# First layer norm as (x − mean)·(1/std) in one two-scalar instruction, 1/std by ln and exp, and a new order of all operations

## Chip, cores, metric

One core of one Trainium2 chip. The metric is the device time of one execution in microseconds (us); lower is better. Ratios of two kernels are the mean time of the one's fast runs over the mean of the other's fast runs of the same rounds, so they are not quite the ratio of the medians that stand beside them. A profiled span is about 1.8 us shorter than the time of the same execution. In lines of the profile PE is TensorE (PEld its weight loads), DVE VectorE, ACT ScalarE and POOL GpSimd; L422 is line 422 of that run's kernel; the number in square brackets is the time that the engine was idle before, and what ended it.

## The reference, cut to what matters

```python
h = _layernorm(x, axis=-1) * (1 + ca) + sa          # first norm: the change is here
x = x + ga * _A_ref(h, A_wqkv, A_w_phi, A_wo)       # linear attention, 32 heads of 16
h = _layernorm(x, axis=-1) * (1 + cb) + sb
x = x + gb * _B_ref(h, B_w_gate, B_w_up, B_w_down)  # silu-gated feed-forward, 512 -> 1376 -> 512
# sa, ca, ga, sb, cb, gb = six parts of silu(c) @ w_mod;  x is 2048 x 512, bf16
# _layernorm: (x - mean) / sqrt(var + 1e-5)
```

The attention needs K and V of all 2048 rows before the first row of its output. So the kernel has a first half (norm, K, V, the K features, their sum over all rows, Q) and a second half (attention output, projection, second norm, feed-forward), which begins when the last of 16 row tiles has gone through the K features.

## The kernel before

The program lists operations with the engines that could do each, and a long list ORDER says in which order and on which engine each is placed; the number beside an engine is the duration in us with which the search for an order reckons. Cut to the parts that matter here:

```python
def rstd_of(mv_t, n, bmv, name, bufs):                 # 1/std and -mean/std, all on GpSimd
    ...
        nc.gpsimd.tensor_scalar_add(neg[:], mv_t()[:, :, 1], LN_EPS)
        nc.gpsimd.tensor_tensor(st["rstd"][:], neg[:], mhalf[:, 0:n], op=ALU.pow)
        ...
            nc.gpsimd.tensor_scalar(neg[:], mv_t()[:, :, 0], -1.0, None, op0=ALU.mult)
            nc.gpsimd.tensor_tensor(st["nmr"][:], neg[:], st["rstd"][:], op=ALU.mult)

def normalize(src, rstd_t, bn, nmr_t, q, reads):       # x * (1/std) + (-mean/std), on one of three engines
    ...
    def fp():
        nc.gpsimd.tensor_scalar(bxn()[:], src, rstd_t()[:, q:q + 1], nmr_t()[:, q:q + 1],
                                op0=ALU.mult, op1=ALU.add)
    pl.op([("DVE*", 0.35, fd), ("ACT", 0.72, fa), ("POOL", 1.11, fp)], r=list(reads) + [bn], w=[bxn])

def k_tile(i):                                         # one row tile of K and V
    ...
    pl.op("POOL", r=[e, R], w=[bphik[i]], us=1.9, fn=lambda: nc.gpsimd.tensor_tensor(   # K features: softmax's division
        bphik[i]()..., e()..., R()[:].unsqueeze(2).to_broadcast([P, 2 * H, DH]), op=ALU.mult))

first_norm(0, 2); ...; first_norm(2, 2); ...           # groups of row tiles: 2, 2, 4, 4, 4
first_norm(4, 4)
first_T(4, 4)
later(wmod_sb[:, :, 2 * D:6 * D], wmod_v[:, :, 2 * D:6 * D])   # 2 MB in one load
```

The softmax here doesn't subtract the row's maximum and nothing guards it: scores larger than these inputs give would overflow.

## Time and profile before

| kernel | median us | lowest to highest | profiled span | clock |
|---|---|---|---|---|
| before | 215.3 (4 runs) | 214.73 to 216.17 | 213.2 | 0.997 |

TensorE bounds the kernel, except for holes in the first 30 us. The prediction shows the lines and how they are read. One more line is needed below, from the groups by shape of the kernel before (columns: line, engine, operation, operands, count, then busy us, mean ns of one, idle before):

```profile
L406 POOL TENSOR_SCALAR xn<-x_c,ln_rstd,ln_nmr 128x512 bf16<-128x512 bf16 x10 | 7.7, 769 | 0.9
```

This is GpSimd's normalization of one row tile: 769 ns.

### The profile page before, as it was taken

How to read it: one execution, taken by the hardware profiler on the slowest of the kernel's cores; microseconds unless marked ns; L12 is line 12 of the kernel's file. 1: busy time of each engine (PE TensorE's matmuls, PEld its weight loads, DVE VectorE, ACT ScalarE, POOL GpSimd, SP SyncE). 2: the span in 40 equal slices, each digit the busy share in tenths (PEclk: the TensorE clock that was granted, in tenths of full speed). 3: DMA queues.
4: the chain of work that ended last, by engine and by line, in shares of the span. 5: the costliest groups of instructions: out<-in, count | busy, mean ns of one | idle time of the engine just before them, and what ended most of it. 6: DMA issues, size and time to landing. Idle time of an engine off the chain costs nothing.

```text
span 213.2 us, 4730 instructions
## 1 busy us (share of the span) xinstructions
PE 200.7 (94%) x1779; PEld 140.2 (66%) x1807; DVE 149.8 (70%) x352; ACT 118.9 (56%) x241; POOL 115.7 (54%) x157
## 2 busy tenths in 40 slices
PE   4997789999999999998999999999999999999993
PEld 1853554555555687786867877777776687777772
DVE  5799969999686977677887596677577764532314
ACT  2677989998889873433533603443342465363230
POOL 5257998899920535672642743654584563441340
PEclk9999999999999999999999999999999999999998
DMA  6996970389600011312221121123211222010001
GB/s 195 363 350 104 389 84 20 71 285 402 217 3 0 0 28 29 74 38 39 54 49 49 39 64 31 46 51 74 52 25 49 51 50 51 28 25 26 28 25 49
DMA packets 30793, 19.24 MB, mean 90 GB/s; under 512 B 22481, under 2 KB 28082, under 8 KB 30770
## 3 DMA queue, kind: packets, MB, share of 16 engines
q1 hardware_dynamic: 30480, 18.85, 31.8%
q8 instruction: 14, 0.23, 0.5%
q10 hardware_dynamic: 290, 0.08, 0.2%
q14 instruction: 9, 0.07, 0.1%
HBM read 11.58 MB, written 2.10 MB: 64 GB/s over the span
## 4 chain that ended last, share of the span: by engine, by line
PE 77%; DMA 13%; SPq 3%; DVE 3%; issue 1%; POOL 1%; DVEq 0%; POOLq 0%
PE one_ps L869 31%; PE one_ps L904 16%; PE one_ps L642 6%; PE one_ps L817 6%; PE one_ps L590 5%; PE one_ps L586 5%; DMA wmod_sb<-in_w_mod_dram 4%; DMA wqkv_sb<-in_A_wqkv_dram 4%; PE four_ps L746 3%; SPq L318 2%; DMA raw<-xn 2%; DMA oT<-o 2%; PE kv_ps L618 2%; DMA wphi_sb<-in_A_w_phi_dram 2%; DVE x_c L820 1%
## 5 line engine op out<-in xcount | busy, mean ns | idle before, releaser
L876 ACT ACTIVATE sg<-one_ps 128x512 bf16<-128x512 f32 (+3 forms) x52 | 27.2, 529 | 44.3 <-PE one_ps L869 39.8
L869 PE MATMUL one_ps<-hT,wu_sb 128*128 128x256 bf16 (+3 forms) x440 | 45.7, 251 | 0.8 <-DVE hT L840 0.8
L869 PE MATMUL one_ps<-hT,wg_sb 128*128 128x256 bf16 (+3 forms) x440 | 44.5, 251 | 0.0
L904 PE MATMUL one_ps<-wd_sb,gu 128*128 128x512 bf16 (+3 forms) x172 | 42.0, 366 | 0.8
L869 PEld LDWEIGHTS <-wu_sb 128*128 128x128 bf16 (+1 forms) x440 | 36.9, 100 | 8.8 <-issue 0.9
L869 PEld LDWEIGHTS <-wg_sb 128*128 128x128 bf16 (+1 forms) x440 | 36.9, 100 | 7.7
L885 POOL TENSOR_TENSOR gu<-usb,sg 128x512 bf16<-128x512 bf16 (+1 forms) x22 | 22.6, 1026 | 22.8 <-ACT sg L876 15.8
L611 POOL TENSOR_TENSOR phik<-e,R 128x1024 bf16<-128x1024 bf16 x16 | 30.6, 1930 | 3.5 <-DVE R L609 2.2
L879 DVE TENSOR_TENSOR gu<-one_ps,sg 128x512 bf16<-128x512 f32 (+2 forms) x30 | 17.8, 595 | 15.9 <-PE one_ps L869 13.0
L904 PEld LDWEIGHTS <-gu 128*128 128x128 bf16 (+1 forms) x187 | 17.8, 98 | 11.9
L375 DVE BATCH_NORM_STATS2 st<-x_c 128x6 f32<-128x512 bf16 x32 | 21.2, 680 | 1.7 <-DMA x_c<-in_A_x_dram 1.4
L883 ACT CAST usb<-one_ps 128x512 bf16<-128x512 f32 (+1 forms) x22 | 11.3, 525 | 18.8 <-PE one_ps L869 15.8
L911 DVE TENSOR_TENSOR fg<-one_ps,gab 128x512 bf16<-128x512 f32 (+1 forms) x17 | 11.2, 656 | 14.8 <-PE one_ps L904 14.5
L804 POOL TENSOR_TENSOR o<-o 128x512 bf16<-128x512 bf16 x14 | 16.2, 1157 | 8.7 <-DVE o L784 8.7
L607 DVE TENSOR_REDUCE S<-e 128x64 f32<-128x1024 bf16 x16 | 19.0, 1194 | 2.2 <-ACT e L597 2.1
L784 DVE TENSOR_TENSOR o<-four_ps,A 128x512 bf16<-128x512 f32 x32 | 20.6, 684 | 0.0
L915 POOL TENSOR_TENSOR ot<-x_c,fg 128x512 bf16<-128x512 bf16 x8 | 9.2, 1154 | 18.5 <-DVE fg L911 18.5
L597 ACT ACTIVATE e<-one_ps 128x512 bf16<-128x512 f32 x32 | 17.3, 607 | 2.7 <-PE one_ps L586 1.7
L648 ACT ACTIVATE eT<-one_ps 128x512 bf16<-128x512 f32 x32 | 17.5, 644 | 1.2 <-PE one_ps L642 1.1
L817 PE MATMUL one_ps<-wo_sb,oT 128*128 128x512 bf16 x60 | 16.2, 379 | 0.5 <-DMA oT<-o 0.3
L820 DVE TENSOR_TENSOR x_c<-x_c,one_ps 128x512 bf16<-128x512 bf16 x16 | 11.0, 687 | 7.5 <-PE one_ps L817 7.2
L590 PE MATMUL one_ps<-wqkv_sb,hT 128*128 128x512 bf16 x62 | 15.8, 379 | 0.1
(102 smaller groups left out, 273.7 us busy)
## 6 DMA issues: line engine op xcount, KB each, us to landing
wmod_sb<-in_w_mod_dram SPq DMA_DIRECT2D x1, 2048.0 KB, 8.2
out_dram<-ot SPq DMA_DIRECT2D x15, 128.0 KB, 1.9
x_c<-in_A_x_dram SPq DMA_DIRECT2D x3, 512.0 KB, 9.4
wg_sb<-in_B_w_gate_dram SPq DMA_DIRECT2D x1, 1376.0 KB, 8.3
wu_sb<-in_B_w_up_dram SPq DMA_DIRECT2D x1, 1376.0 KB, 11.2
wd_sb<-in_B_w_down_dram SPq DMA_DIRECT2D x1, 1280.0 KB, 14.4
wmod_sb<-in_w_mod_dram SPq DMA_DIRECT2D x4, 256.0 KB, 5.0
wqkv_sb<-in_A_wqkv_dram SPq DMA_DIRECT2D x2, 512.0 KB, 7.8
```

What stands on the lines that cost most here:

```text
L375: pl.op("DVE", r=reads, w=[st6], us=0.6, fn=lambda: nc.vector.bn_stats(st6()[:], src))
L590: nc.tensor.matmul(v()[:], lhsT=hT[c_i][k][:, cols], rhs=wqkv_sb[:, k, 2 * D:3 * D], start=(k == 0), stop=(k == KD - 1))
L607: pl.op("DVE", r=[e], w=[Ss], us=1.14, fn=lambda: nc.vector.tensor_reduce(Ss()[:], e()[:].rearrange("p g s h f -> p (g s h) f"), axis=AX.X ...
L611: pl.op("POOL", r=[e, R], w=[bphik[i]], us=1.9, fn=lambda: nc.gpsimd.tensor_tensor(bphik[i]()[:].rearrange("p g s h f -> p (g s h) f"), e( ...
L648: pl.op("ACT", r=[pq, btab], w=[beT[c_i, sg, j]], us=0.48, fn=lambda sg=sg: nc.scalar.activation(eTs[c_i, sg, j][:], pq()[:], ACT.Exp, sca ...
L784: nc.vector.tensor_tensor(o2()[:, sg].rearrange("p j (h d) -> p j h d", d=DH), ndv()[:, :, sg, 0:P].rearrange("p j (h d) -> p j h d", d=DH ...
L817: nc.tensor.matmul(a()[:], lhsT=oT()[:, j, :], rhs=wo_sb[:, j, :], start=(j == 0), stop=(j == KD - 1))
L869: nc.tensor.matmul(ps_()[0:fsz, q * n:(q + 1) * n], lhsT=wt[:, k, m * P:m * P + fsz], rhs=h2[k], start=(k == 0), stop=(k == KD - 1))
L876: pl.op("ACT", r=[g, btab], w=[sg], us=0.08 + 0.41 * L / CW, fn=lambda: nc.scalar.activation(sg()[0:fsz, 0:L], g()[0:fsz, 0:L], ACT.Silu))
L879: pl.op("DVE", r=[u, sg], w=[gu], us=0.07 + 0.535 * L / CW, fn=lambda: nc.vector.tensor_tensor(gu()[0:fsz, 0:L], u()[0:fsz, 0:L], sg()[0:f ...
L885: pl.op("POOL", r=[usb, sg], w=[gu], us=0.05 + 1.06 * L / CW, fn=lambda: nc.gpsimd.tensor_tensor(gu()[0:fsz, 0:L], usb()[0:fsz, 0:L], sg() ...
L904: nc.tensor.matmul(fp()[:], lhsT=b()[0:fsz, c0:c0 + P], rhs=wd_sb[0:fsz, m, cs], start=(m == 0), stop=(m == FM - 1))
```

## The change

The intent: take the first norm's small instructions off GpSimd (ln and exp on ScalarE give 1/std, and no −mean/std is needed if the mean is subtracted first), take the normalizing itself off ScalarE, let row tiles 4 to 7 go on in pairs, split a 2 MB load, and search a new order with re-fitted durations. Core of the diff (QUOTA limits how many buffers of a kind the order may hold, and PAIRS lists the groups of four row tiles that go on in pairs; the 948 numbers of ORDER become 954 others; further re-fitted constants, changed fillers, the rest of the load bookkeeping and the removal of an unused path are cut):

```diff
-QUOTA = {'q': 3, 'turn': 4, 'T': 2, 'T2': 2, 'wo': 4, 'down': 3, 'gu': 2, 'kv': 4, 'fold': 4}
+QUOTA = {'q': 9, 'turn': 9, 'T': 9, 'T2': 9, 'wo': 9, 'down': 9, 'gu': 9, 'kv': 9, 'fold': 9}
+PAIRS = (0, 1)
...
+    nc.scalar.add_instruction(mybir.InstLoadActFuncSet(name=..., act_func_set_id=6, ins=[], outs=[]))
...
+    def rstd_lnexp(mv, n, bmv, name):
+        ...
+        def fa():
+            nc.scalar.activation(var[:], mv[:, :, 1], ACT.Ln, bias=eps_t[:])
+            nc.scalar.activation(rstd[:], var[:], ACT.Exp, scale=-0.5)
+        def fp():
+            nc.gpsimd.tensor_scalar_add(var[:], mv[:, :, 1], LN_EPS)
+            nc.gpsimd.tensor_tensor(rstd[:], var[:], mhalf[:, 0:n], op=ALU.pow)
+        pl.op([("ACT", 0.8, fa), ("POOL", 0.9 + 0.1 * n, fp)], r=bmv, w=[b])
+    def center(src, mv, rstd, b, q, reads):
+        ...
+        def f(eng):
+            eng.tensor_scalar(bxn()[:], src, mv[:, q, 0:1], rstd[:, q:q + 1], op0=ALU.subtract, op1=ALU.mult)
+        pl.op([("DVE*", 0.35, lambda: f(nc.vector)), ("POOL", 0.78, lambda: f(nc.gpsimd))], r=list(reads) + [b], w=[bxn])
...
-    first_norm(4, 4)
-    first_T(4, 4)
+    first_norm(4, 2)
+    first_T(4, 2)
+    first_norm(6, 2)
+    first_T(6, 2)
...
-    later(wmod_sb[:, :, 2 * D:6 * D], wmod_v[:, :, 2 * D:6 * D])
+    for i in range(2):
+        cols = slice((2 + 2 * i) * D, (4 + 2 * i) * D)
+        later(wmod_sb[:, :, cols], wmod_v[:, :, cols], [], [bm2[i]])
```

## The prediction

> **What bounds the kernel now.** I read the page's busy shares first:
>
> ```profile
> PE 200.7 (94%) x1779; PEld 140.2 (66%) x1807; DVE 149.8 (70%) x352; ACT 118.9 (56%) x241; POOL 115.7 (54%) x157
> ```
>
> TensorE is the engine to save on, but 94% includes the filler matmuls (the line L978), which only multiply ones. So the second view is the table of windows (stretch, busy us of PE, PEld, DVE, ACT and POOL with counts, clock, DMA share, GB/s):
>
> ```profile
> 10.00:20.00 10.00, 8.80 (x57) 4.59 (x59) 9.48 (x25) 7.44 (x15) 6.07 (x9) 1.00 0.93 257
> 20.00:30.00 10.00, 8.10 (x83) 5.14 (x83) 8.88 (x20) 9.09 (x16) 9.27 (x12) 1.00 0.94 251
> 40.00:50.00 10.00, 9.95 (x81) 5.28 (x81) 9.68 (x13) 10.00 (x20) 9.51 (x7) 1.00 0.79 262
> 170.00:190.00 20.00, 19.90 (x156) 15.21 (x157) 9.50 (x22) 10.96 (x21) 9.16 (x14) 1.00 0.19 41
> ```
>
> The reader is to see that from 40 us on TensorE is full, while between 10 and 30 us the other three engines are at 75 to 95% and TensorE is not. The timeline of TensorE between 15 and 31 us (start, us, engine, line, operands, count, idle before) shows what is missing:
>
> ```profile
> 15.26 0.38 PE L978 MATMUL kv_ps<-ones 128*128 128x512 bf16 x1
> 15.47 0.61 PE L419 MATMUL one_ps<-ident_b,xn 128*128 128x128 bf16 x8
> ...
> 17.84 0.40 PE L523 MATMUL one_ps<-BD,WT 128*128 128x128 bf16 x4 [1.11 <-ACT hT L427]
> 18.08 0.59 PE L978 MATMUL kv_ps<-ones 128*128 128x512 bf16 x2
> 18.51 1.03 PE L586 MATMUL one_ps<-Wk,hT 128*128 128x512 bf16 x4
> ...
> 24.36 0.61 PE L419 MATMUL one_ps<-ident_b,xn 128*128 128x128 bf16 x8
> 24.81 0.83 PE L978 MATMUL kv_ps<-ones 128*128 128x252 bf16 x6
> 27.37 0.55 PE L464 MATMUL one_ps<-silucT,wmod_sb 128*128 128x1 bf16 x16 [1.73 <-DMA wmod_sb<-in_w_mod_dram]
> ```
>
> Two holes: 15.3 to 18.5 us (tiles 2 and 3 are not yet transposed and modulated) and 23.3 to 27.4 us. In the second, row tiles 4 to 7 become usable only as a group of four, and the next matmuls in order stand behind the 2 MB second load of w_mod, issued at 19.14 and landed at 27.3. By 27.4 TensorE has done K and V of only four tiles. From there to the last matmul at 209.7 us I add up about 2.2 us of idle and 0.65 us of fillers (the waits of TensorE and three 216 ns fillers at 69 to 74 us), most of it between 68 and 99 us. The last 3.5 us are the final evacuation and store.
>
> The middle has a second limit. The timeline of GpSimd shows the K features going one after the other until the attention can start:
>
> ```profile
> 49.11 9.47 POOL L611 TENSOR_TENSOR phik<-e,R 128x1024 bf16<-128x1024 bf16 x5 [0.25 <-PE one_ps L586]
> ```
>
> That is 1.9 us a tile, 16 tiles, with little idle from 24 us on; the last key-value matmuls (57.8 to 59.1 us) wait for it. So a gain in front stays only if GpSimd is brought forward too.
>
> **What the Trainium skill says.** "ScalarE: Activation LUTs", section "Table sets: the hidden batching unit": ln and exp lie together in one named set, so going from one to the other needs no second load; its section "What ACT_TABLE_LOAD costs" gives about 1283 ns for a load. The trace agrees on the load: two, 1283 ns each (before the first exp, and before silu). The change loads one set by hand at the start; if that is the common set, the count stays two. "GPSIMD Engine Reference", section 3.1, has 769 ns measured for a one-input loop over 512 elements; GpSimd's normalize here takes 769 ns (L406, x10), so the cost model's old 1.11 us was wrong and the new 0.78 right. The same page, section 1, says GpSimd shares its SBUF interfaces with VectorE, with contention for instructions in a two-port mode; the trace shows VectorE's normalize between 314 and 405 ns, not enough to prove it.
>
> **The change part by part.** The order lists name an operation and its engine in each number; counting the operations in program order decodes them, so I could read the new order per engine. It is all rearranged, so costs are taken from present rows.
>
> (1) First norm. Now five groups each run four small GpSimd instructions: about 1.8 us for two tiles (6.90 to 8.59) and 2.0 for four, five groups 9.6 us. Afterwards six groups (tiles 4 to 7 split into pairs); two stay on GpSimd with two instructions (0.24 + 0.73 and gaps, 1.05 us each, 2.1 us), four go to ScalarE as ln and exp (about 0.8 us each by the listed cost; the 128x4 exp here takes 0.17 us, so most is hand-over). Normalizing: now 5 tiles on GpSimd, 9 on ScalarE, 2 on VectorE; afterwards 11, 0 and 5. GpSimd gets 6 x 0.77 = +4.6 us, loses 7.5 us and one modulation (0.8): net about -3.7. ScalarE loses 9 x about 0.74 = 6.7 us and gets 3.2: net -3.5. VectorE gets 3 x 0.36, about +1. The subtraction form costs the same as the multiply-add.
>
> (2) Pairs for tiles 4 to 7, x and w_mod loads in halves, new order. I walked the new order by hand. The first K matmul stays near 11.6 us (now 11.79): it waits for w_mod's first 1 MB, whose last quarter is used at 9.55. ScalarE does ln and exp of tiles 2 and 3 before the first K exponentials, 12.9 to 13.6; two exponential pairs and a V copy (1.06 + 1.06 + 0.55) end at 16.2; the two evacuations (0.97 each) at 18.2. So the first hole stays: tile 3 starts near 18.4 against 18.5. From there the new TensorE order is: four K/V (0.865 each), transposes of 6 and 7, the first key-value product, a fold, to 23.2; tile 6's evacuation on ScalarE ends near 23.0. Then K6, V7, K7 to 26.1, K4 at 26.35, and gate 0 at 27.2, which needs only the first half of w_mod (landing about 24, an estimate: half of 8.2 us after 19.6). V5, K5, V4, the modulation columns, V6 and gate 1 follow without a hole to 34.1, where K8 starts. Now K8 starts at 37.19. The work ahead of it is the same: one gate more (0.865) and one Q block less, and two modulation steps more (0.25). Sum: 37.19 - 34.1 + 0.25 = 3.3 us of holes removed.
>
> (3) GpSimd's chain by the same walk: its features of tiles 1, 3 and 2 end near 30.4, tile 4's at 34.3, then 11 x 1.93 ends near 55.5 against 58.6 now. That is 3.1 us earlier, so it follows TensorE nearly in full. Eight Q blocks precede the first attention matmul in both orders, eight follow it.
>
> (4) After that TensorE's work is the same instruction for instruction. What can still be won is the 2.85 us of idle and fillers. The new order pulls attention matmuls further ahead of their users, but the start looks alike: tile 2's output needs about 8 us from attention matmul to projection (vector work, a 1.16 us add, a 4.1 us transpose), with 7.6 us of other work placed there, a hole of about 0.4 as now (0.29). I allow 0.8 us of the 2.85 to go.
>
> (5) Removed, no effect on the end: the unused late path, quotas, the changed fillers (they only take up holes).
>
> Sum: 215.4 - 3.3 - 0.8 = 211.3 us, 1.9% faster.
>
> **Rivals.** (a) ScalarE becomes the bound in front. By my walk it is busy without pause from 12.9 to 34 us, with tile 6 ready at 23.0 for use at 23.2. Half a microsecond of slip there, or a table load of 1.28 us before every ln, goes straight to the end. For it: 9.1 of 10 us busy now. Against: it sheds 3.5 us. One extra pair of loads would leave 1 us less gain, a pair per group eats all of it: 212.5 to 216. (b) Off the path: the holes close, but GpSimd's features take over and the saved time is waited out before the attention, because 11 normalizations now stand in their queue. For it: the 9.47 us row. Then the gain is only what GpSimd sheds late: 213 to 214. (c) The new order also removes nearly all later idle: 215.4 - 3.3 - 2.3 = 209.8. For it: no limit on buffers of one kind and re-fitted costs. Against: an order is planned with one fixed transpose time (1.3 us plus hand-over), where this trace has 2.4 to 4.4.
>
> **Range and chances.** The centre is 211.3. My hand walk may be off by 1 us in front (chains of ten rounded durations) and the later idle by 1 us; together about 1.5 us: 8 in 10 between 209.4 and 213.3. The line for 2% is 211.1, so it is nearly even: faster 0.46, same 0.52, slower 0.02, the last for repeated table loads or an order that fits badly.
>
> **What would show it.** Right: no filler or idle over 0.3 us on TensorE between 18.4 and 34 us; K8's first matmul at 34 (now 37.2); the last GpSimd feature ending at 55 to 56; first attention matmul near 58.2 (now 61.5); two table loads; ScalarE without normalizations of the first norm; about 2 us of idle after 60. Wrong: a hole at 22 to 27 us with ScalarE as its releaser (a); TensorE idle or filled just before the attention with GpSimd still busy (b); a first hole at 15 to 18.4 us that is much shorter, which would mean that I misplaced the evacuations and the gain is above 4 us.

## The result, and the profile after

| kernel | median us | lowest to highest | ratio to before (95%) | span | clock |
|---|---|---|---|---|---|
| before | 215.3 (4 runs) | 214.73 to 216.17 | | 213.2 | 0.997 |
| changed | 223.9 (4 runs) | 223.81 to 224.27 | 1.040 (1.036 to 1.044) | 222.5 | 0.985 |

The kernel became 4.0% slower where 1.9% faster was predicted. The busy shares of the changed kernel, then the windows that answer to those of before:

```profile
PE 207.5 (93%) x1819; PEld 141.5 (64%) x1819; DVE 142.2 (64%) x333; ACT 117.7 (53%) x251; POOL 134.6 (60%) x162
```

```profile
10.00:20.00 10.00, 8.52 (x48) 4.24 (x49) 5.91 (x15) 4.43 (x11) 8.40 (x15) 0.83 0.82 261
20.00:30.00 10.00, 7.23 (x52) 3.60 (x50) 8.31 (x21) 6.27 (x16) 9.95 (x5) 1.00 0.60 210
30.00:40.00 10.00, 6.56 (x50) 3.66 (x51) 3.79 (x9) 5.76 (x12) 10.00 (x6) 0.99 0.29 55
40.00:50.00 10.00, 10.00 (x96) 5.15 (x94) 8.97 (x16) 9.49 (x20) 7.90 (x6) 0.84 0.30 66
```

GpSimd was to lose 3.7 us and has gained 18.9. It is busy for 19.95 of the 20 us from 20 to 40, while all other engines have slack: ScalarE, which was at 9.99 of 10 us from 30 to 40, is at 5.76. In the timeline of GpSimd one sees with what (start, us, instruction, count):

```profile
7.28 4.15 POOL L422 TENSOR_SCALAR xn<-x_c,ln_mv,ln_rstd 128x512 bf16<-128x512 bf16 x2
...
14.79 4.13 POOL L422 TENSOR_SCALAR xn<-x_c,ln_mv,ln_rstd 128x512 bf16<-128x512 bf16 x2 [1.38 <-ACT ln_rstd L409]
...
20.05 4.14 POOL L422 TENSOR_SCALAR xn<-x_c,ln_mv,ln_rstd 128x512 bf16<-128x512 bf16 x2
24.16 1.93 POOL L640 TENSOR_TENSOR phik<-e,R 128x1024 bf16<-128x1024 bf16 x1
26.07 10.29 POOL L422 TENSOR_SCALAR xn<-x_c,ln_mv,ln_rstd 128x512 bf16<-128x512 bf16 x5
36.32 5.70 POOL L640 TENSOR_TENSOR phik<-e,R 128x1024 bf16<-128x1024 bf16 x3
```

Two normalizations take 4.1 us, not 1.5. The group of that line:

```profile
L422 POOL TENSOR_SCALAR xn<-x_c,ln_mv,ln_rstd 128x512 bf16<-128x512 bf16 x11 | 22.7, 2075 | 1.6 <-ACT ln_rstd L409 1.4
```

2075 ns against 769 ns in the kernel before: 11 × 1.306 = 14.4 us more than planned, on the engine whose chain leads to the attention. (The new order also gives GpSimd 12 modulations of the second norm, L877, 6.4 us, which the prediction did not count; the runs of experiments 1 and 5 have them too.) The timeline of TensorE shows where this arrives:

```profile
11.48 0.40 PE L449 MATMUL one_ps<-ident_b,xn 128*128 128x128 bf16 x4 [2.34 <-POOL xn L422]
...
30.25 0.34 PE L449 MATMUL one_ps<-ident_b,xn 128*128 128x128 bf16 x3 [1.83 <-POOL xn L422]
...
38.31 0.43 PE L647 MATMUL kv_ps<-va,phik 128*128 128x65 bf16 x8 [2.73 <-POOL phik L640]
...
46.74 1.03 PE L615 MATMUL one_ps<-Wk,hT 128*128 128x512 bf16 x4
...
68.13 0.43 PE L647 MATMUL kv_ps<-va,phik 128*128 128x65 bf16 x8 [0.15 <-POOL phik L640]
...
70.98 0.66 PE L779 MATMUL four_ps<-KVZ,eT 128*128 128x144 bf16 x8
```

Every new hole of more than half a microsecond before the attention is released by GpSimd, by a normalization or by a feature queued behind one. The last two landmarks in the kernel before:

```profile
37.19 1.03 PE L586 MATMUL one_ps<-Wk,hT 128*128 128x512 bf16 x4
...
61.50 0.66 PE L746 MATMUL four_ps<-KVZ,eT 128*128 128x144 bf16 x8
```

K of tile 8 starts at 46.74 us (37.19 before), the first attention matmul at 70.98 (61.50 before): 9.5 us later, and the span is 9.3 us longer. So all of the loss is made in the first half.

There are two ACT_TABLE_LOADs as before, 1283 ns each: that part of the prediction held.

### The profile page after: what moved, and what is told of

Its sections match the earlier page's. It is cut to its first block, busy times and chain, and to the rows that moved or that the text cites. A ratio compares the mean times of both kernels' runs of the same rounds, so it can differ in the third digit from the quotient of the medians.

```text
span 222.5 us, 4784 instructions
## 1 busy us (share of the span) xinstructions
PE 207.5 (93%) x1819; PEld 141.5 (64%) x1819; DVE 142.2 (64%) x333; ACT 117.7 (53%) x251; POOL 134.6 (60%) x162
## 4 chain that ended last, share of the span: by engine, by line
PE 65%; POOL 9%; ACT 8%; DMA 8%; issue 4%; SPq 3%; DVE 2%; POOLq 0%; ACTq 0%; DVEq 0%
PE one_ps L904 32%; PE one_ps L939 16%; PE one_ps L850 6%; POOL phik L640 5%; POOL xn L422 4%; ACT eT L677 3%; DMA wqkv_sb<-in_A_wqkv_dram 3%; PE four_ps L779 3%; PE one_ps L615 2%; PE one_ps L619 2%; PE one_ps L671 2%; ACT e L626 2%; DMA oT<-o 2%; SPq L320 2%; DMA wphi_sb<-in_A_w_phi_dram 2%
## 5 line engine op out<-in xcount | busy, mean ns | idle before, releaser
L904 PE MATMUL one_ps<-hT,wg_sb 128*128 128x256 bf16 (+3 forms) x440 | 45.5, 251 | 0.4 <-ACT hT L457 0.4
L904 PE MATMUL one_ps<-hT,wu_sb 128*128 128x256 bf16 (+3 forms) x440 | 45.0, 251 | 0.0
L939 PE MATMUL one_ps<-wd_sb,gu 128*128 128x512 bf16 (+3 forms) x187 | 43.0, 367 | 0.0
L422 POOL TENSOR_SCALAR xn<-x_c,ln_mv,ln_rstd 128x512 bf16<-128x512 bf16 x11 | 22.7, 2075 | 1.6 <-ACT ln_rstd L409 1.4
L391 POOL TENSOR_SCALAR ln_neg<-ln 128x1 f32<-128x1 f32 x16 | 3.5, 219 | 27.8 <-DVE ln L381 27.1
L918 ACT CAST usb<-one_ps 128x512 bf16<-128x512 f32 (+1 forms) x22 | 11.5, 524 | 14.4 <-PE one_ps L904 9.8
L615 PE MATMUL one_ps<-Wk,hT 128*128 128x512 bf16 x64 | 17.9, 410 | 0.0
```

Source lines behind the costliest of these rows:

```text
L422: eng.tensor_scalar(bxn()[:], src, mv[:, q, 0:1], rstd[:, q:q + 1], op0=ALU.subtract, op1=ALU.mult)
L615: nc.tensor.matmul(pk()[:], lhsT=hT[c_i][k][:, cols], rhs=Wk2[:, k, :], start=(k == 0), stop=(k == KD - 1))
L904: nc.tensor.matmul(ps_()[0:fsz, q * n:(q + 1) * n], lhsT=wt[:, k, m * P:m * P + fsz], rhs=h2[k], start=(k == 0), stop=(k == KD - 1))
L939: nc.tensor.matmul(fp()[:], lhsT=b()[0:fsz, c0:c0 + P], rhs=wd_sb[0:fsz, m, cs], start=(m == 0), stop=(m == FM - 1))
```

## The experiments

The theory after this reading (A): the form, subtract then multiply, is slow on GpSimd. Rivals: (B) the operands, because the mean is read out of a strided statistics tile, or VectorE is on the shared ports; (C) the new order is bad in itself.

### 1. Multiply and add on the same operands

```diff
-            eng.tensor_scalar(bxn()[:], src, mv[:, q, 0:1], rstd[:, q:q + 1], op0=ALU.subtract, op1=ALU.mult)
+            eng.tensor_scalar(bxn()[:], src, rstd[:, q:q + 1], mv[:, q, 0:1], op0=ALU.mult, op1=ALU.add)
```

> The changed kernel, with the 16 normalizations of the first norm as (x times 1/std) plus mean, a multiply then an add, instead of (x minus mean) times 1/std. Same tiles as operands, same engines, same order; the result is wrong by twice the mean over std on purpose (some hundredths). Theory A, the form (subtract, then multiply) is what makes GpSimd slow: the 11 GpSimd normalizations go from 2.07 to about 0.77 us, their chain gives back 14 us, the rest of the prediction holds, and the time is 209.4 to 213.3 us. Theory B, the operands do it (a mean read out of a strided statistics tile, or VectorE on the shared ports): they stay near 2.07 us and the time near 224. Theory C, the new order is bad in itself: 0.77 us each, but over 216 us.

Measured: 212.87 us median (211.82 to 213.28, 4 runs), ratio 0.988 (0.984 to 0.992). GpSimd's normalizations:

```profile
L422 POOL TENSOR_SCALAR xn<-x_c,ln_rstd,ln_mv 128x512 bf16<-128x512 bf16 x11 | 8.4, 772 | 3.2 <-ACT ln_rstd L409 3.0
```

(The result is wrong, by so little that the comparison with the reference still passed.) Two operators exchanged, with the same tiles, engines and order: 11 us. This speaks against B and against C. (One oddity of this run was not tested: VectorE's modulation L584, 0.31 us in the changed kernel, took 1.99 us here, beginning 0.09 us after a GpSimd feature of 1.93 us.)

### 2. Eleven forms by themselves

At the end of the kernel before, each form twice, in one execution. In the second round (from 221.2 us) GpSimd is alone; beside the first, VectorE still has three additions (208.2 to 209.9 us):

```diff
+    probe = const.tile([P, D], BF16, name="probe")
+    xs, s1, s2 = x_ch[0][:, 0, :], modB[:, 0:1], modB[:, 1:2]
+        nc.gpsimd.tensor_scalar(probe[:], xs, s1, s2, op0=ALU.mult, op1=ALU.add)           # L987
+        nc.gpsimd.tensor_scalar(probe[:], xs, s1, s2, op0=ALU.subtract, op1=ALU.mult)      # L988
+        nc.gpsimd.tensor_scalar(probe[:], xs, s1, s2, op0=ALU.add, op1=ALU.mult)           # L989
+        nc.gpsimd.tensor_scalar(probe[:], xs, s1, s2, op0=ALU.mult, op1=ALU.subtract)      # L990
+        nc.gpsimd.tensor_scalar(probe[:], xs, s1, s2, op0=ALU.mult, op1=ALU.mult)          # L991
+        nc.gpsimd.tensor_scalar(probe[:], xs, s1, s2, op0=ALU.add, op1=ALU.add)            # L992
+        nc.gpsimd.tensor_scalar(probe[:], xs, s1, None, op0=ALU.subtract)                  # L993
+        nc.gpsimd.tensor_scalar(probe[:], xs, s1, None, op0=ALU.mult)                      # L994
+        nc.gpsimd.tensor_scalar(probe[:], xs, 0.5, 2.0, op0=ALU.subtract, op1=ALU.mult)    # L995
+        # L996, L997: subtract-multiply and multiply-add on 256 columns
```

> The kernel before, followed at its end by eleven forms of GpSimd's two-scalar instruction on the same 128x512 bf16 tile with nothing beside them, twice each; only their durations count. Theory A: multiply-add 0.77 us, subtract-multiply 2.07 us with plain, unstrided scalars and VectorE idle; half the columns give about half. Open is which part is slow: if add-multiply is 2.07 too, it is every pair but multiply-add; if only the pairs with a subtraction, it is the subtraction. Theory B: all pairs about 0.77 us here.

The instructions that write this tile (shortest/median/longest ns, first and last start, form):

```profile
L987 POOL TENSOR_SCALAR probe<-x_c,modB x2: 759/763/767, 204.5 to 221.2; 128x512 bf16<-128x512 bf16 x2
L988 POOL TENSOR_SCALAR probe<-x_c,modB x2: 2072/2086/2101, 205.4 to 222.1; 128x512 bf16<-128x512 bf16 x2
L989 POOL TENSOR_SCALAR probe<-x_c,modB x2: 767/767/767, 207.6 to 224.3; 128x512 bf16<-128x512 bf16 x2
L990 POOL TENSOR_SCALAR probe<-x_c,modB x2: 2082/2193/2304, 208.4 to 225.1; 128x512 bf16<-128x512 bf16 x2
L991 POOL TENSOR_SCALAR probe<-x_c,modB x2: 767/769/771, 210.8 to 227.3; 128x512 bf16<-128x512 bf16 x2
L992 POOL TENSOR_SCALAR probe<-x_c,modB x2: 2085/2100/2115, 211.7 to 228.2; 128x512 bf16<-128x512 bf16 x2
L993 POOL TENSOR_SCALAR probe<-x_c,modB x2: 1567/1568/1569, 213.9 to 230.4; 128x512 bf16<-128x512 bf16 x2
L994 POOL TENSOR_SCALAR probe<-x_c,modB x2: 1562/1562/1562, 215.6 to 232.0; 128x512 bf16<-128x512 bf16 x2
L995 POOL TENSOR_SCALAR probe<-x_c x2: 1932/1932/1932, 217.2 to 233.7; 128x512 bf16<-128x512 bf16 x2
L996 POOL TENSOR_SCALAR probe<-x_c,modB x2: 1213/1213/1213, 219.3 to 235.7; 128x256 bf16<-128x256 bf16 x2
L997 POOL TENSOR_SCALAR probe<-x_c,modB x2: 548/548/549, 220.6 to 237.0; 128x256 bf16<-128x256 bf16 x2
```

Multiply-add, add-multiply and multiply-multiply take 0.77 us; subtract-multiply, multiply-subtract and also add-add take 2.07 to 2.09 in the second round (the shortest values). The starts bear the durations out: L988 begins 0.9 us after L987, and L989 2.2 us after L988. So it is not the subtraction as such: three pairs are fast, and the three others tried are not. A single multiply (1.56 us) takes twice as long as the fast pair that contains it. The scalars are plain here, and in the second round VectorE is not beside it, which ends B. (The one long value, 2304 ns, is of the first round, while VectorE's additions ran; the second time the same form took 2082.) From 256 to 512 columns the slow form grows, by the medians, by 873 ns and the fast one by 215 (3.4 and 0.84 ns a column): the slow form is slow per element. (At 256 columns it therefore takes 58% of the time at 512, not half as I expected.) Why GpSimd has two speeds is not visible in a trace and stays open.

### 3. The slow form put into the kernel before

```diff
         def fp():
+            if mv is not None:      # first norm only
+                nc.gpsimd.tensor_scalar(bxn()[:], src, mv[:, q, 0:1], rstd_t()[:, q:q + 1], op0=ALU.subtract, op1=ALU.mult)
+                return
             nc.gpsimd.tensor_scalar(... op0=ALU.mult, op1=ALU.add)
```

> The kernel before, unchanged but for the five first-norm tiles that GpSimd normalizes (3, 2, 7, 9, 12): subtract and multiply instead of multiply and add; correct result. Theory A: each goes from 0.77 to 2.07 us, 5 x 1.3 = 6.5 us more on GpSimd, which has little idle from 24 to 59 us; tiles 3 and 2 also lengthen the first hole by 2.6. Time 218 to 222 us. If it stays within 216, the slow form costs only together with the new order (11 tiles).

Measured: 217.67 us (217.52 to 218.13, 4 runs), ratio 1.011 (1.007 to 1.015). The harm comes without the new order too, but the time is under the expected 218 to 222. TensorE waits 2.16 us for a normalization before the second transposes, and the K product after them starts at 21.16 us instead of 18.51: 2.65 us later, about the 2.6 us of the two tiles in front of it. Nothing of the other three tiles' 3.9 us is seen in the end.

### 4. All sixteen normalizations on VectorE

```diff
-        pl.op([("DVE*", 0.35, lambda: f(nc.vector)), ("POOL", 0.78, lambda: f(nc.gpsimd))], ...)
+        pl.op([("DVE*", 0.35, lambda: f(nc.vector)), ("POOL", 0.78, lambda: f(nc.vector))], ...)
```

> The changed kernel with the first norm's 16 normalizations all on VectorE, in the form subtract and multiply (correct result), places in the order kept. GpSimd loses 11 x 2.07 = 22.8 us and VectorE gets 11 x about 0.35 = 4 us more. Theory A and B both: GpSimd's chain is free; VectorE was 95% busy before between 10 and 30 us and now takes 0.35 us where the plan had 0.78 on GpSimd. Expected 210 to 215 us. Theory C (the order is bad in itself): over 216.

Measured: 212.49 us (212.38 to 214.51, 4 runs), ratio 0.990 (0.984 to 0.995). Subtract and multiply take 428 ns on VectorE in the mean, with no penalty like GpSimd's: the slow form belongs to one engine.

### 5. Two mends with a correct result

(a) minus mean over std by VectorE, then multiply and add:

```diff
         def f(eng):
-            eng.tensor_scalar(bxn()[:], src, mv[:, q, 0:1], rstd[:, q:q + 1], op0=ALU.subtract, op1=ALU.mult)
+            if "nmr" not in st:     # once a group
+                st["nmr"] = lnp.tile([P, st["n"]], FP32, name=st["name"] + "_nmr")
+                nc.vector.scalar_tensor_tensor(st["nmr"][:], in0=mv[:, :, 0], scalar=-1.0, in1=rstd[:], op0=ALU.mult, op1=ALU.mult)
+            eng.tensor_scalar(bxn()[:], src, rstd[:, q:q + 1], st["nmr"][:, q:q + 1], op0=ALU.mult, op1=ALU.add)
```

> A mend with a correct result: minus mean over std by one small VectorE instruction per group (six of about 0.16 us), then multiply and add on the engines of the changed kernel. Theory A: normalizations on GpSimd 0.77 us, time as in the run with the wrong result plus up to 1 us (a VectorE instruction that waits for 1/std in order). That is 210 to 214 us, faster than both kernels. Theory B or C: over 216.

Measured: 211.82 us (210.32 to 212.12, 4 runs), ratio 0.982 (0.977 to 0.987). Timed again, with the changed kernel on the same chip:

> The mended kernel (multiply and add, minus mean over std by VectorE) a second time, with five rounds, for its interval against the kernel before: 211 to 212.5 us, ratio 0.98 to 0.987. Against the changed kernel of the same job it should be 12 us less.

> The changed kernel as it is, beside the run with fillers and the mended one on the same chip: 223.9 us, within 0.5.

Measured: 212.03 us (210.73 to 212.33, 6 runs), ratio to before 0.984 (0.979 to 0.988), and 223.52 us (222.55 to 224.06, 4 runs) for the changed kernel. The mend is 11.5 us under the changed kernel and faster than both; that it is faster than before by more than 2% is not settled.

(b) minus mean made beside 1/std (ScalarE four times, GpSimd twice), then add and multiply:

```diff
+            nc.scalar.activation(neg[:], mv[:, :, 0], ACT.Identity, scale=-1.0)                 # where ln and exp are
+            nc.gpsimd.tensor_scalar(neg[:], mv[:, :, 0], -1.0, None, op0=ALU.mult)              # where the power is
...
+            eng.tensor_scalar(bxn()[:], src, mv[1][:, q:q + 1], rstd[:, q:q + 1], op0=ALU.add, op1=ALU.mult)   # mv[1] is neg
```

> Another mend with a correct result: minus mean is made beside 1/std on the engine of that step (one more small instruction, about 0.2 us, ScalarE four times, GpSimd twice), then add and multiply, which the run of forms has at 0.77 us on GpSimd. No hand-over to VectorE. Theory A: 0.77 us each, 210 to 212.5 us, at or a little below the mend with multiply and add (211.8).

Measured: 213.01 us (211.47 to 213.83, 6 runs), ratio 0.988 (0.984 to 0.992). The median is above the expected 210 to 212.5, and not below mend (a); as a form, add-multiply is as fast as multiply-add in experiment 2.

The landmarks of mend (a), from the timeline of TensorE and then of GpSimd:

```profile
34.54 1.03 PE L619 MATMUL one_ps<-Wk,hT 128*128 128x512 bf16 x4
...
58.96 0.66 PE L783 MATMUL four_ps<-KVZ,eT 128*128 128x144 bf16 x8
```

```profile
48.46 7.59 POOL L644 TENSOR_TENSOR phik<-e,R 128x1024 bf16<-128x1024 bf16 x4
```

K of tile 8 starts at 34.54 us, the last feature ends at 56.05 and the attention begins at 58.96.

### 6. Was the slower clock of TensorE part of the loss?

In single microseconds, the changed kernel's trace has TensorE's granted clock at 0.50 from 13 to 15 us and from 40 to 43, after holes of 2.34 and 2.73 us; with the parts of the microseconds beside them each slow spell is about 3.4 us long. The skill's page "TensorE: Matmul & The Clock Gate", Part 1, says that the array falls to half rate after an idle window of about 3.4 us and needs some 3.4 us of work to come back. The way back agrees (about 3.4 us); the holes that were enough here were shorter. Filler matmuls put into both holes:

```diff
+            left += 10 * CW if o.n == 44 else 0                                                    # before the first transposes
-            fns += [lambda: f(n)] * int((o.start - t0 - 0.1) * FILL / each)
+            fns += [lambda: f(n)] * (int((o.start - t0 - 0.1) * FILL / each) + (25 if o.n == 128 else 0))   # before the second key-value product
```

> The changed kernel with its slow GpSimd form, but with filler matmuls put into TensorE's two longest holes (10 of 512 columns before the first transposes, 2.2 us; 25 of 252 before the second key-value product, 2.7 us); correct result. After each of these holes the trace of the changed kernel has TensorE at clock 0.5 for some 3.3 us. If that clock is part of the loss: no window under 0.95, and the time 1.5 to 3 us under that of the changed kernel run beside it (223.9), so 221 to 222.4. If GpSimd's chain is the bound all the way to the attention, the slow clock is hidden behind it: within 0.7 us of 223.9.

Windows of the run with fillers, then of the changed kernel (the clock is the third number from the end):

```profile
30.00:35.00 5.00, 4.90 (x25) 2.56 (x26) 3.03 (x8) 3.04 (x7) 5.00 (x4) 0.69 0.26 57
35.00:40.00 5.00, 5.00 (x50) 3.88 (x49) 0.73 (x1) 2.90 (x6) 5.00 (x4) 1.00 0.25 52
40.00:45.00 5.00, 5.00 (x69) 2.98 (x67) 4.26 (x11) 4.97 (x11) 3.25 (x3) 1.00 0.16 35
```

```profile
30.00:35.00 5.00, 4.75 (x31) 2.51 (x32) 3.19 (x8) 4.04 (x8) 5.00 (x4) 1.00 0.32 57
35.00:40.00 5.00, 1.81 (x21) 1.15 (x20) 0.60 (x1) 1.72 (x4) 5.00 (x3) 0.99 0.25 53
40.00:45.00 5.00, 5.00 (x59) 2.57 (x57) 4.34 (x8) 4.49 (x10) 3.25 (x3) 0.67 0.12 28
```

222.74 us (222.51 to 222.97, 4 runs) against 223.52 (222.55 to 224.06) beside it: the medians differ by 0.8, the ranges overlap, and the time lies between the two that were expected. Both slow spells are gone, but another came at 30 us, after a hole of 1.83 us; the changed kernel's trace has a hole of 1.83 us at the same place, and no slow spell after it. So the profiled run is not a clean test. GpSimd is full in both from 30 to 40 us.

The mean clocks say more. A spell of 3.4 us at 0.50 takes 3.4 × 0.5 / 222 = 0.008 from the mean, so 0.985 means two spells, as in the changed kernel's trace, 0.992 one, as in the trace with fillers, and 0.998 none. Of the changed kernel's four runs beside the fillers, the one with 0.992 took 222.55 us and the three with 0.985 took 223.4 to 224.06. Of the four runs with fillers, the one with 0.998 took 222.51 us and the three with 0.992 took 222.57 to 222.97. In experiment 3 two runs with 1.000 (217.52 and 218.13 us) and two with 0.992 (217.61 and 217.72) do not differ. So the slow clock is worth about 1 us of the loss, as far as single executions show; in the one execution without a slow spell nearly all of it was still there.

### 7. What ln and exp are worth

With mend (a), but all six 1/std by power on GpSimd; and, the other way round, the kernel before with that part alone:

```diff
-        pl.op([("ACT", 0.8, fa), ("POOL", 0.9 + 0.1 * n, fp)], r=bmv, w=[b])      # in mend (a)
+        pl.op([("ACT", 0.8, fp), ("POOL", 0.9 + 0.1 * n, fp)], r=bmv, w=[b])
```

> The mended kernel (multiply and add, minus mean over std on VectorE) with all six 1/std on GpSimd by power, none by ln and exp on ScalarE: worth of that part. GpSimd gets four times 1.0 to 1.3 us, ScalarE loses four times 0.5 us. If ln and exp carry the gain: 213.5 to 216 us. If only the pairs and the order carry it: within 1 us of the mended kernel, 211 to 213.

```diff
+            if n > 1:       # in the kernel before, first norm; the set loaded by hand at the start is cut
+                nc.scalar.activation(neg[:], mv_t()[:, :, 1], ACT.Ln, bias=eps_t[:])
+                nc.scalar.activation(st["rstd"][:], neg[:], ACT.Exp, scale=-0.5)
+                nc.gpsimd.tensor_scalar(neg[:], mv_t()[:, :, 0], -1.0, None, op0=ALU.mult)
+                nc.gpsimd.tensor_tensor(st["nmr"][:], neg[:], st["rstd"][:], op=ALU.mult)
+                return
```

> The kernel before with that part alone: 1/std of the five first-norm groups by ln and exp on ScalarE (one table set loaded by hand, two table loads in all), the rest and the order as before. GpSimd loses 5 x 1.0 to 1.3 us, ScalarE, full from 30 to 50 us, gets 5 x 0.5. The holes of TensorE come from grouping and order, so 214 to 216 us; below 213.5 would mean that this part alone makes the gain.

Measured: 214.50 us (213.48 to 214.62, 4 runs), ratio 0.995 (0.991 to 0.999), for the first; 215.27 us (215.16 to 216.84, 4 runs), ratio 1.002 (0.997 to 1.007), for the second. Without ln and exp most of the mended kernel's gain of 3 us is gone; alone they bring nothing. The parts pay together. The first number flatters ln and exp somewhat: in that run VectorE's small instruction for minus mean over std waits 2.35 us in its queue for GpSimd's power, a wait that the mend itself brought in.

## Why the prediction was wrong

**The step that failed** is one sentence in part (1): "The subtraction form costs the same as the multiply-add." It took 769 ns from the row of the kernel before, where every such GpSimd instruction is multiply-add, and gave it to another pair of operators. (That a page of the skill has 769 ns too made the listed 0.78 look confirmed; but the page has it for the best case of a tight loop over 512 elements, and names neither this pair nor, as the prediction does, one input.) Measured: 2075 ns. The term of the sum, "6 x 0.77 = +4.6 us", would have been 11 × 2.075 − 5 × 0.77 = +19.0 us, and GpSimd's net not −3.7 but +10.7. Part (3) has GpSimd's chain open the attention, 3.1 us earlier than before; 14.4 us more on that chain give a slower kernel by the same walk. The cost model in the change made the same step: it lists 0.78 us for the new form.

**What held, given the 0.77 us.** The mended kernel is what I had predicted on paper, and its trace follows the walk: no hole over 0.3 us on TensorE from 18.57 to 34.54 us (predicted 18.4 to 34), K of tile 8 at 34.54 (34.1), the last feature at 56.05 (55.5), the attention at 58.96 (58.2), two table loads, no first-norm normalization on ScalarE. Its 211.8 and 212.0 us stand against the predicted 211.3.

**Part (4), the later idle**, stays open. From 60 to 110 us TensorE is busy for 48.52 us in the kernel before, 0.65 of them with fillers. In the mended kernel's first trace it is 47.99 us without fillers, so hardly anything of the 0.8 us allowed was won; in its second trace (experiment 5, timed again, 210.73 us) it is 49.38, so more than that was. Of the ten mended runs three took 211.1 us or less and seven 211.5 to 212.4; what decides between them was not looked for.

**Small misreadings** that change nothing: the four small GpSimd instructions of a pair take 1.7 us (6.90 to 8.59), not 1.8, and VectorE's longest normalization is 415 ns, not 405.

**The rivals.** (a) ScalarE as the bound: not seen; in the changed kernel it has slack. (b) GpSimd's chain takes over: this came, through a longer instruction and not through the queueing that I gave as its reason, and so far stronger than its 213 to 214 us. (c) was not reached: the fastest mended run took 210.32 us against its 209.8. The chance of 0.02 for slower named table loads and a bad order; the real cause was on no list.

**What the prediction could have said.** No row of the profile shows a subtract-multiply on GpSimd, and no page that I read gives its cost. The 2.7 to 1 between two pairs could not be known; that the form had never been measured here, and that 11 of them would stand on the critical chain, could. That deserved a rival and a wider range.

## What to carry to other kernels

A duration from a profile belongs to an operation with its operators, dtype and engine; when a change alters one of them, the cost is unknown until measured, and an instruction that will stand on the critical chain is worth a one-line probe first. A form that is simpler on paper (one operation fewer) can be the dearer one: here 2.07 against 0.77 us on GpSimd for a 128x512 bf16 tile. So on GpSimd write (x − mean)/std as multiply-add or add-multiply, and leave subtract-multiply to VectorE. When a search places operations by a cost model, one wrong entry can load the engine that only looks cheap: here 11 of 16 tiles went to GpSimd at a listed 0.78 us.

## What the Trainium skill lacked or had wrong

- "GPSIMD Engine Reference", section 3.1, gives 769 ns, as the best case of a tight loop, for 512 elements and no difference between pairs of operators. Here GpSimd's two-scalar instruction on 128x512 bf16 took 0.77 us for multiply-add, add-multiply and multiply-multiply, 2.07 to 2.09 us for subtract-multiply, multiply-subtract and add-add, 1.93 us for subtract-multiply with immediates, and 1.56 us for a single multiply or subtract: one operation alone takes twice as long as the fast pair.
- "TensorE: Matmul & The Clock Gate", Part 1, has half rate after an idle window of about 3.4 us. Here shorter holes were enough: those of 2.34 and 2.73 us were each followed by about 3.4 us at clock 0.50. Nor did the length alone decide: a hole of 1.83 us was followed by such a spell in the run with fillers and not in the changed kernel, and one of 1.73 us in the kernel before was not.
